# Four of the sixteen up units of a block as seven products of sums, in a fused retention and MLP kernel

## The chip, the cores and the metric

The kernel runs on one core of a Trainium2 chip. The metric is the device time of one execution in microseconds (us), lower is better. Its engines, each with its own queue of instructions in a fixed order: TensorE (PE in the profile; PEld are its weight loads), VectorE (DVE), ScalarE (ACT), GpSimd (POOL) and SyncE (SP), which here only issues DMA transfers.

## The reference

Retention over 8 batches, 8 heads, 576 steps of 64 features, and behind it an MLP with a hardswish on the 4608 rows that come out. Cut to what matters:

```python
scores = scale * np.matmul(q, k.transpose(0, 1, 3, 2))
Dmat = np.where(rel >= 0, gamma[:, None, None] ** rel[None, :, :], 0.0)
ret = np.matmul(scores * Dmat[None], v)
x = ret.transpose(0, 2, 1, 3).reshape(B * S, H * D)      # 4608 x 512
h = x @ w_in                                             # 512 x 2048
g = h * np.clip(h + 3.0, 0.0, 6.0) / 6.0
out = g @ w_out                                          # 2048 x 512
```

## The kernel before

The rows are worked off in nine blocks of 512 (block 0 gathers the first 64 steps of every batch, blocks 1 to 8 are the rest of one batch each). A block has three parts of work on TensorE:

- Attention, in chunks of 128 rows, in 64 x 64 tiles. It gives the block's transposed input `xts[kb]`, 512 features x 512 rows, in f16. Chunks have steps with letters: `c` casts a chunk's k, q and v to f16 (k on ScalarE, q and v on GpSimd, L188 to L195), then issues the transposing DMAs and the loads of a later chunk on SP's queue; `a` scores, `s` state sums, `u` adds to the running state (two additions on VectorE, L313 and L316, then a scaling by GpSimd, L317), `z` casts a state to f16 on ScalarE (L323), `x` and `i` multiply and copy the result into `xts`.
- Up: 16 units. A unit is 128 of the 2048 columns of h for all 512 rows: 4 products of 512 columns (`up_steps`, L491). Its result lies in one PSUM bank; ScalarE makes u = relu(h/6 + 0.5) from it (L510), and VectorE g = min(u, 1) * h (L512).
- Down: from block 2 on (`down_strassen`, L562) the product with w_out is made by the scheme of Strassen in Winograd's form: 7 products of half the size in each direction instead of 8, from sums of parts of g (side sums, L527, on VectorE, taken from a list by the step `+`) and sums of parts of w_out that are made once (`ws`). This comes to 112 TensorE products of 256 columns a block. The results of the seven are copied from PSUM by ScalarE or combined by VectorE and GpSimd; two of the banks take a second product on top of the first once the first has been copied. The copy that the prediction follows is `nc.scalar.copy(u2, bc)` (L631 before, L712 in the changed kernel), after down product 6 and before down product 7 is added to the same bank.

What `product` issues is two matmuls, one for each half of the 128 output partitions, so a product is two matmul instructions in the profile.

The order of instructions is written out by hand. In the loop over kb from 2 (L811) the up units of block kb + 1, the down products of block kb and the attention steps for later blocks are interleaved: before unit 0 come 5 down products, behind each unit 7 (less those that were taken ahead), and a table by unit number, `STEADY` (L710), says which steps stand behind which unit: for instance 4 chunk c4 is cast; behind 5 come 7 more down products and the steps a2, x0, s2, i0, u2; c6 stands behind 12, z3 behind 8. `FIRST_STEADY` does so for kb = 2.

[...] An instruction on any engine waits, in order, until the bank or buffer that it writes is free.

At the start, before data has come, TensorE runs idle products (`idle_products`, L375): 11 products of 512 columns on the identity, in four groups between the first transposes.

Of the kernel before, what the change touches and what calls it, by code (L numbers as in the profile page):

```python
# [21 lines left out]
def kernel(  # L22
# [21 lines left out]
    JQ = 4  # L44
    HB = BLK // 2
    FIRST = 2
    HM = DM // 2
# [39 lines left out]
    zh = [const.tile([P, NP, D], FP32, name=f"zh{b}") for b in range(B)]  # L87
# [61 lines left out]
    def product(out, lhs, rhs, **flags):  # L149

        for h2 in range(2):
            r = slice(h2 * D, h2 * D + D)
            nc.tensor.matmul(out[r], lhs[:, r], rhs, skip_group_check=True, **flags)  # L153
# [333 lines left out]
    def up_unit(kb, u, th=None):  # L487
        for _ in up_steps(kb, u, th):
            pass
# [47 lines left out]

    def out_tile(kb, m2):
        return work.tile([P, 2, DM], FP32, tag=f"o{m2}", bufs=2, name=f"o{m2}_{kb}")

    kept = deque()

# [149 lines left out]
    def go(plan, kb=None, down=None):  # L692
# [3 lines left out]
        for item in plan.split():  # L696
# [9 lines left out]
            else:  # L706
# [3 lines left out]
    STEADY = {0: [("u", 1)], 1: [("z", 1), ("+", 1)], 2: [("+", 1)], 4: [("c", 4)],  # L710
# [4 lines left out]

# [6 lines left out]

    with tc.manual_schedule(engines={ENG.PE, ENG.DVE, ENG.Pool, ENG.Activation, ENG.SP}):
# [25 lines left out]
        idle_products(5)  # L749
# [5 lines left out]
        idle_products(4)  # L755
# [9 lines left out]
        idle_products(1)  # L765
# [4 lines left out]
        idle_products(1)  # L770
# [24 lines left out]
        for u in range(4, NFC):  # L795
# [14 lines left out]
           2, down)  # L810
        for kb in range(2, NB):  # L811
            for _ in down:
                pass
            plain = kb < FIRST
            down = down_plain(kb) if plain else down_strassen(kb)
            per = 4 if plain else 7
            table = FIRST_STEADY if kb == 2 else STEADY
            c = NCB * (kb + 2)
            owed = 0
            for u in range(NFC):  # L820
                if u == 0:
                    owed += per - 2
                    for _ in range(per - 2):
# [5 lines left out]
                owed -= per  # L829
                while owed < 0:  # L830
                    next(down, None)
                    owed += 1
                for w, i in table.get(u, []):
                    if w == "D":
                        for _ in range(i):
                            next(down, None)
                        owed += i
                    else:
                        do([(w, i if w == "+" else c + i)])
# [32 lines left out]
```

## Time and profile before

| what | value |
|---|---|
| median of three runs | 299.51 us (298.39 to 301.02) |
| the profiled execution | 301.02 us |
| its span, first to last instruction | 299.3 us |
| granted TensorE clock, mean | 1.000 |
| TensorE, busy from 180 to 200 us | 20.00 of 20.00 us |
| VectorE, the same stretch | 14.36 us |
| ScalarE, the same stretch | 13.33 us |
| GpSimd, the same stretch | 8.96 us |
| TensorE, busy from 0 to 20 us | 15.63 us |

The profile is of one execution, the longest of the three. A group of instructions is named by its line, engine and operation, what it writes and reads, and its shape (partitions x elements and type); behind the bar stand its busy time, the mean duration of one instruction in ns, and the idle time of the engine just before, with what ended it. In a timeline the first two numbers are the start and the length in us; in the chain of waits too, where each piece is a stretch of work that the end of the run was waiting for. Matmuls are pipelined, and their ends are modelled.

### The profile page before, as it was taken

How to read it: one execution, taken by the hardware profiler on the slowest of the kernel's cores; microseconds unless marked ns; L12 is line 12 of the kernel's file. 1: busy time of each engine (PE TensorE's matmuls, PEld its weight loads, DVE VectorE, ACT ScalarE, POOL GpSimd, SP SyncE). 2: the span in 40 equal slices, each digit the busy share in tenths (PEclk: the TensorE clock that was granted, in tenths of full speed). 3: DMA queues.
4: the chain of work that ended last, by engine and by line, in shares of the span. 5: the costliest groups of instructions: out<-in, count | busy, mean ns of one | idle time of the engine just before them, and what ended most of it. 6: DMA issues, size and time to landing. Idle time of an engine off the chain costs nothing.

```text
span 299.3 us, 12661 instructions
## 1 busy us (share of the span) xinstructions
PE 287.4 (96%) x5574; PEld 219.3 (73%) x5574; DVE 216.2 (72%) x388; ACT 193.9 (65%) x360; POOL 133.7 (45%) x170
## 2 busy tenths in 40 slices
PE   4999998999999999999999999999999999999995
PEld 2776644777556667888777878778778987778894
DVE  7749545669897778788967797688869776647654
ACT  3748854799866696686677577667766574565420
POOL 8971057526762920719631962386247003100510
PEclk9999999999999999999999999999999999999999
DMA  6999999998999999997999999999906100200114
GB/s 157 157 182 213 186 227 209 227 228 183 161 216 164 249 202 191 178 239 195 225 220 225 169 201 216 150 177 247 148 3 142 72 2 30 102 15 2 72 72 140
DMA packets 119542, 47.86 MB, mean 160 GB/s; under 512 B 92352, under 2 KB 114880, under 8 KB 119488
## 3 DMA queue, kind: packets, MB, share of 16 engines
q1 hardware_dynamic: 114336, 41.56, 71.1%
q0 software_dynamic: 4720, 5.11, 10.5%
q8 instruction: 43, 0.70, 1.0%
q10 hardware_dynamic: 432, 0.39, 0.5%
q14 instruction: 11, 0.09, 0.1%
HBM read 36.70 MB, written 9.44 MB: 154 GB/s over the span
## 4 chain that ended last, share of the span: by engine, by line
PE 79%; DMA 9%; POOL 6%; SPq 2%; ACT 2%; issue 1%; DVE 1%; POOLq 0%; ACTq 0%
PE ph L153 37%; PE pm L153 29%; DMA wout<-in_moe_w_out_dram 6%; PE pd L153 5%; PE po L231 4%; DMA fq<-in_q_dram 2%; PE pa L231 2%; SPq L174 2%; POOL hv L439 1%; POOL hk L399 1%; POOL win L658 1%; PE pu L231 1%; POOL ws L741 1%; PE ptk L153 1%; POOL q L192 1%
## 5 line engine op out<-in xcount | busy, mean ns | idle before, releaser
L153 PE MATMUL ph<-xT,win 128*64 128x512 f16 (+1 forms) x1248 | 144.8, 364 | 1.2 <-DMA win<-in_moe_w_in_dram 0.5
L512 DVE SCALAR_TENSOR_TENSOR g<-u,ph 128x512 f16<-128x512 f32 (+1 forms) x156 | 98.8, 643 | 53.1 <-ACT u L510 52.6
L510 ACT ACTIVATE u<-ph,half 128x512 f32<-128x512 f32 (+1 forms) x156 | 100.5, 659 | 43.0 <-PE ph L153 40.6
L153 PEld LDWEIGHTS <-win 128*64 128x64 f16 x1248 | 82.9, 136 | 28.6 <-DMA win<-in_moe_w_in_dram 1.1
L153 PEld LDWEIGHTS <-g 128*64 128x64 f16 x928 | 51.1, 110 | 14.9 <-issue 0.4
L153 PEld LDWEIGHTS <-s 128*64 128x64 f16 x896 | 50.3, 110 | 8.1 <-issue 0.2
L317 POOL TENSOR_TENSOR z<-z,gpow 128x256 f32<-128x256 f32 x24 | 15.8, 657 | 69.1 <-DVE z L316 51.2
L153 PE MATMUL pm<-ws,s 128*64 128x256 f16 x672 | 45.6, 273 | 0.0
L192 POOL TENSOR_TENSOR q<-fq,dec 128x512 f16<-128x512 f32 x32 | 36.7, 1166 | 3.4 <-DVE zh L282 1.7
L369 ACT CAST xT<-po 128x256 f16<-128x256 f32 (+1 forms) x44 | 22.5, 583 | 23.4 <-PE po L231 22.5
L195 POOL TENSOR_TENSOR v<-fv,dec 128x512 f16<-128x512 f32 x32 | 35.4, 1111 | 2.1 <-DMA fv<-in_v_dram 2.1
L591 POOL TENSOR_TENSOR u<-u,p 128x512 f32<-128x512 f32 x7 | 8.9, 1271 | 60.4 <-ACT u L631 54.2
L153 PE MATMUL pd<-wout,g 128*64 128x512 f16 x256 | 34.7, 382 | 0.1
L153 PE MATMUL pm<-wout,g 128*64 128x256 f16 x448 | 31.1, 273 | 0.0
L266 DVE TENSOR_TENSOR a<-pa,mask 128x256 f16<-128x256 f32 (+1 forms) x44 | 21.9, 539 | 8.4 <-PE pa L231 4.7
L188 ACT CAST k<-fk 128x512 f16<-128x512 f32 x32 | 19.9, 622 | 2.1 <-DMA fk<-in_k_dram 2.1
L527 DVE TENSOR_TENSOR s<-g 128x1024 f16<-128x1024 f16 x28 | 19.3, 692 | 0.2
L323 ACT CAST z<-z 128x512 f16<-128x512 f32 x24 | 14.9, 622 | 5.1 <-DVE z L313 4.7
L153 PE MATMUL pm<-ws,g 128*64 128x256 f16 x224 | 16.7, 274 | 0.0
L153 PE MATMUL pm<-wout,s 128*64 128x256 f16 x224 | 16.3, 273 | 0.1
L527 DVE TENSOR_TENSOR s<-g,s 128x1024 f16<-128x1024 f16 x14 | 13.3, 949 | 0.0
L231 PE MATMUL po<-qT,z 64*64 64x64 f16 x512 | 12.5, 198 | 0.4 <-ACT z L326 0.3
(106 smaller groups left out, 270.0 us busy)
## 6 DMA issues: line engine op xcount, KB each, us to landing
fk<-in_k_dram SPq DMA_DIRECT2D x32, 256.0 KB, 4.6
fq<-in_q_dram SPq DMA_DIRECT2D x16, 512.0 KB, 6.0
fv<-in_v_dram SPq DMA_DIRECT2D x32, 256.0 KB, 5.5
out_dram<-o SPq DMA_DIRECT2D x14, 512.0 KB, 3.8
wout<-in_moe_w_out_dram POOLq DMA_DIRECT2D x4, 512.0 KB, 17.9
out_dram<-o SPq DMA_DIRECT2D x7, 256.0 KB, 5.4
win<-in_moe_w_in_dram POOLq DMA_DIRECT2D x3, 512.0 KB, 10.9
hq<-in_q_dram SPq DMA_DIRECT2D x6, 128.0 KB, 4.6
```

The source lines that it names most:

```text
L153: nc.tensor.matmul(out[r], lhs[:, r], rhs, skip_group_check=True, **flags)
L188: nc.scalar.copy(by_head(k16), in_rows(st[c]["fk"]))
L192: nc.gpsimd.tensor_tensor(by_head(q16[:, e]), in_rows(st[c]["fq"][:, :, e, :]), in_rows(dd[:, 2 + e, 0:H, :]), ALU.mult)
L195: nc.gpsimd.tensor_tensor(v16, st[c]["fv"], dd[:, 1, H:2 * H, :], ALU.mult)
L231: return lambda: nc.tensor.matmul(*args, skip_group_check=True, **flags)
L266: nc.vector.tensor_tensor(a16[:, a, 0:n].rearrange("p x i q -> p (x i) q"), pa[a].rearrange("p x i q -> p (x i) q"), m, ALU.mult)
L317: nc.gpsimd.tensor_tensor(new, new, decay, ALU.mult)
L323: nc.scalar.copy(z16, zs[c])
L369: nc.scalar.copy(xt[:, s], po[s].rearrange("p x n (e r) -> p x n e r", e=2))
L510: nc.scalar.activation(uu[:, 0:n], ph[:, 0:n], ACTF.Relu, bias=half, scale=1.0 / 6.0)
L512: nc.vector.scalar_tensor_tensor(out=g[:, hf, ths, jr, :], in0=by_half(uu), scalar=1.0, in1=by_half(ph), op0=ALU.min, op1=ALU.mult)
L527: nc.vector.tensor_tensor(*pend.popleft())
```

## The change

From kb = 3 to kb = 7, that is for the up parts of blocks 4 to 8, units 8 to 11 (the first four with `jq` = 1) are made together, as a quad. The 512 x 512 part of w_in and the 512 x 512 input are each cut in 2 x 2, and the seven products of Strassen's method in Winograd's form take the place of the eight block products. Each of the seven is four products of 256 columns. The 64 products of 512 columns of a block's up part become 48 of 512 and 28 of 256.

- `sums_of_w` makes four sums of parts of w_in once, on GpSimd, behind unit 14 of kb = 2 (step `W`). They lie in a part of `wout16` that is no longer read.
- `sums_of_x` makes four sums of parts of `xts` in each of the five blocks, on GpSimd (step `T`, behind u1 and z1).
- `up_quad` is a generator with six stretches, called by `Q1` and five times `q` in `PLAN`, which takes the place of the table `STEADY` for these blocks. It uses three banks (x, z, y), of which x and y are added to after they have been copied to `p` and `q` in SBUF by ScalarE.
- In the order, c6 moves from behind unit 12 to behind the first stretch of the quad, and z3 from behind unit 8 to behind the fifth, and the side sums move among the new stretches.
- The first of the two output tiles has one buffer in place of two, and one tile more of its kind, `late_out`, holds the first output tile of block 1 and then the sums of x. `zh` becomes one tile, of which a part holds `q` of the quad. `query` moves into a tile that exists already.
- The idle products have 80 columns in place of 512, and there are 24, 19, 5 and 5 in place of 5, 4, 1 and 1.
- kb = 2 and kb = 8 keep their order.

```diff
-    query = const.tile([P, P], FP32)
-    dist, far = early[:, 0:P], early[:, P:2 * P]
+    dist, far, query = early[:, 0:P], early[:, P:2 * P], early[:, 2 * P:3 * P]
...
-        idle = psum.tile([P, NP, P], FP32, tag="pp", name="idle")
+        idle = psum.tile([P, 80], FP32, tag="pp", name="idle")
         for _ in range(n):
-            product(idle, ident16, ident16.unsqueeze(1).to_broadcast([P, NP, P]), start=True, stop=True)
+            product(idle, ident16, ident16[:, 0:80], start=True, stop=True)
...
+    late_out = const.tile([P, 2, DM], FP32)
     def out_tile(kb, m2):
-        return work.tile([P, 2, DM], FP32, tag=f"o{m2}", bufs=2, name=f"o{m2}_{kb}")
+        return late_out if (kb, m2) == (1, 0) else work.tile([P, 2, DM], FP32, tag=f"o{m2}", bufs=1 + m2, name=f"o{m2}_{kb}")
...
+    def sums_of_w(jq):
+        w, (s1, s2, s3, s4) = w_of(jq), [w_sums[:, n] for n in range(4)]
+        a11, a12, a21, a22 = [w[:, 2 * k:2 * k + 2, JP * i:JP * i + JP] for i in range(2) for k in range(2)]
+        for o, x, y, op in ((s1, a21, a22, ALU.add), (s2, s1, a11, ALU.subtract), (s3, a11, a21, ALU.subtract),
+                            (s4, a12, s2, ALU.subtract)):
+            for c in range(2):
+                nc.gpsimd.tensor_tensor(o[:, c], x[:, c], y[:, c], op)
+
+    def sums_of_x(kb):
+        b11, b12, b21, b22 = [xts[kb][:, 2 * k:2 * k + 2, HB * t:HB * t + HB] for k in range(2) for t in range(2)]
+        t1, t2, t3, t4 = [x_sums[:, n] for n in range(4)]
+        nc.gpsimd.tensor_tensor(t1, b12, b11, ALU.subtract)
+        nc.gpsimd.tensor_tensor(t2, b22, t1, ALU.subtract)
+        nc.gpsimd.tensor_tensor(t3, b22, b12, ALU.subtract)
+        nc.gpsimd.tensor_tensor(t4, b21, t2, ALU.subtract)
+
+    def gate(kb, g, src):
...
+        nc.scalar.activation(u, src, ACTF.Relu, bias=half, scale=1.0 / 6.0)
+        nc.vector.scalar_tensor_tensor(out=g, in0=u, scalar=1.0, in1=src, op0=ALU.min, op1=ALU.mult)
+
+    def up_quad(kb, jq):
...
+        plain = lambda i, k: (lambda c, j: w[:, 2 * k + c, JP * i + j, :])
+        summed = lambda n: (lambda c, j: w_sums[:, n - 1, c, j, :])
+        x = lambda k, t: (lambda c: xts[kb][:, 2 * k + c, HB * t:HB * t + HB])
+        xs = lambda n: (lambda c: x_sums[:, n - 1, c, :])
...
+        def one(n, lhs, rhs, more=False):
+            for j in range(JP):
+                for c in range(2):
+                    product(b[n][:, j, :], lhs(c, j), rhs(c), start=(c == 0 and j == 0 and not more), stop=(c == 1))
+
+        b["x"] = bank("x")
+        one("x", plain(0, 0), x(0, 0))
+        nc.scalar.copy(p, b["x"])
+        b["z"] = bank("z")
+        one("z", plain(0, 1), x(1, 0))
+        nc.vector.tensor_tensor(b["z"], b["z"], p, ALU.add)
+        yield
+        b["y"] = bank("y")
+        one("y", summed(1), xs(1))
+        nc.scalar.copy(q, b["y"])
+        one("x", summed(2), xs(2), True)
+        nc.scalar.copy(p, b["x"])
+        gate(kb, g[:, 0, 0:JP], b["z"])
+        yield
+        one("y", summed(4), x(1, 1), True)
+        nc.vector.tensor_tensor(b["y"], b["y"], p, ALU.add)
+        yield
+        one("x", summed(3), xs(3), True)
+        nc.scalar.copy(p, b["x"])
+        gate(kb, g[:, 1, 0:JP], b["y"])
+        nc.gpsimd.tensor_tensor(q, q, p, ALU.add)
+        yield
+        one("x", plain(1, 1), xs(4), True)
+        gate(kb, g[:, 0, JP:JQ], b["x"])
+        yield
+        gate(kb, g[:, 1, JP:JQ], q)
+        yield
...
-    STEADY = {0: [("u", 1)], 1: [("z", 1), ("+", 1)], 2: [("+", 1)], 4: [("c", 4)],
-              5: [("D", 7), ("a", 2), ("x", 0), ("s", 2), ("i", 0), ("u", 2)], 6: [("c", 5), ("u", 3), ("+", 1)],
-              7: [("z", 2), ("+", 1)], 8: [("z", 3)], 9: [("+", 1)], 10: [("+", 1)],
-              12: [("c", 6)], 13: [("D", 6), ("a", 4), ("x", 2), ("s", 4), ("i", 2), ("u", 4), ("D", 1)],
-              14: [("c", 7), ("z", 4), ("+", 1)], 15: [("+", 1)]}
+    PLAN = ("D5 U0 D2 u1 U1 D7 z1 T +1 U2 D7 +1 U3 D7 U4 D7 c4 U5 D14 a2 x0 s2 i0 u2 "
+            "U6 c5 u3 +1 U7 D7 z2 +1 Q1 c6 D6 q D7 q +1 D5 q +1 D6 U12 q z3 D9 q U13 D15 a4 x2 s4 i2 u4 D1 "
+            "U14 z4 c7 +1 U15 D7 +1")
...
-        idle_products(5)
+        idle_products(24)
...
+            if SIDE <= kb < NB - 1:
+                steady(kb, down)
+                continue
```

In `PLAN`, `D` is so many down products of block kb, `U` an up unit of block kb + 1, `Q` and `q` the stretches of the quad, `T` the sums of x, and the other letters are the steps above.

More of the change, by code (lines that the diff above doesn't have):

```diff
@@ L86 @@
     gpow = const.tile([P, NP], FP32)
-    zh = [const.tile([P, NP, D], FP32, name=f"zh{b}") for b in range(B)]
+    states_of_heads = const.tile([P, B, NP, D], FP32)
+    zh = [states_of_heads[:, b] for b in range(B)]
     def indices():
@@ new lines, in sums_of_x @@
+    def sums_of_x(kb):
[6 more added lines that the diff above has]
+    def gate(kb, g, src):
+        u = work.tile([P, BLK], FP32, tag="u", bufs=3, name=f"u{kb}")
+        u = u.rearrange("p (j t) -> p j t", j=JP)
+        nc.scalar.activation(u, src, ACTF.Relu, bias=half, scale=1.0 / 6.0)
+        nc.vector.scalar_tensor_tensor(out=g, in0=u, scalar=1.0, in1=src, op0=ALU.min, op1=ALU.mult)
@@ L810, with steady @@
            2, down)
+        def steady(kb, down):
+            c0 = NCB * (kb + 2)
+            u, quad = 0, None
+            for item in PLAN.split():
+                what, n = item[0], int(item[1:] or 0)
+                if what == "D":
+                    for _ in range(n):
+                        next(down, None)
+                elif what == "U":
+                    up_unit(kb + 1, n)
+                elif what == "Q":
+                    quad = up_quad(kb + 1, n)
+                    next(quad)
+                elif what == "q":
+                    next(quad)
+                elif what == "T":
+                    sums_of_x(kb + 1)
+                else:
+                    do([(what, n if what == "+" else c0 + n)])
         for kb in range(2, NB):
@@ L813 @@
                 pass
[L814 to L817, printed above, removed]
+            down = down_strassen(kb)
+            if SIDE <= kb < NB - 1:
+                steady(kb, down)
+                continue
+            table = FIRST_STEADY if kb == 2 else {}
             c = NCB * (kb + 2)
@@ L821 @@
                 if u == 0:
-                    owed += per - 2
-                    for _ in range(per - 2):
+                    owed += 5
+                    for _ in range(5):
                         next(down, None)
@@ L828 @@
                     side_sums(1)
-                owed -= per
+                owed -= 7
                 while owed < 0:
```

23 lines of the change are left out of this document (20 added, 3 removed), and 2 rows, old and new, of the table FIRST_STEADY.

## The prediction

> **What bounds the kernel now.** I read the page first, for the busy shares:
>
> ```profile
> PE 287.4 (96%) x5574; PEld 219.3 (73%) x5574; DVE 216.2 (72%) x388; ACT 193.9 (65%) x360; POOL 133.7 (45%) x170
> ```
>
> TensorE is busy nearly all the time, and no other engine comes near it. Busy is not the same as paced, so I read the chain of waits next, inside the stretch that the change rewrites (start, length, what):
>
> ```profile
> 213.35 0.76 PE pm L153 x14
> 214.12 0.86 PE ph L153 x8
> 214.98 0.77 PE pm L153 x14
> 215.74 0.86 PE ph L153 x8
> ```
>
> From 72 us to 294 us the chain is almost nothing but such pieces, end to end: an up unit (8 matmuls, 4 products of 512 columns) takes 0.864 us, seven down products of 256 columns take 0.765 us. So a product costs 0.216 us at 512 columns and 0.1093 us at 256. What is taken off TensorE here comes off the end, and each microsecond in which TensorE waits is added. The chain before 50 us runs through GpSimd's DMA issues, the w_out transfer and the q load, not through TensorE.
>
> Third, the timeline where the quad is put (block kb = 5; the first unit that it replaces starts at 213.95, my t = 0), ScalarE, VectorE and GpSimd by themselves:
>
> ```profile
> 212.76 0.69 ACT L510 ACTIVATE u<-ph,half 128x512 f32<-128x512 f32 x1
> 213.33 0.62 ACT L188 CAST k<-fk 128x512 f16<-128x512 f32 x1
> 213.84 0.70 ACT L510 ACTIVATE u<-ph,half 128x512 f32<-128x512 f32 x1
> 214.42 0.63 ACT L323 CAST z<-z 128x512 f16<-128x512 f32 x1
> ```
>
> ```profile
> 214.09 0.42 DVE L313 TENSOR_TENSOR z<-pu,z 128x256 f32<-128x256 f32 x1
> 214.42 0.68 DVE L527 TENSOR_TENSOR s<-g 128x1024 f16<-128x1024 f16 x1
> 215.02 0.68 DVE L512 SCALAR_TENSOR_TENSOR g<-u,ph 128x512 f16<-128x512 f32 x1
> 215.62 0.69 DVE L527 TENSOR_TENSOR s<-g 128x1024 f16<-128x1024 f16 x1
> 216.22 0.68 DVE L512 SCALAR_TENSOR_TENSOR g<-u,ph 128x512 f16<-128x512 f32 x1
> ```
>
> ```profile
> 212.83 0.61 POOL L317 TENSOR_TENSOR z<-z,gpow 128x256 f32<-128x256 f32 x1 [3.99 <-DVE z L316]
> ```
>
> ScalarE and VectorE work off a queue here: the relu at 213.84 belongs to a unit whose matmuls were done at 213.35. Back to back, an instruction starts before the one ahead of it ends, by 0.12 us on ScalarE (a relu of 0.69 is followed after 0.57) and 0.09 on VectorE (0.69, after 0.60).
>
> Fourth, the groups that price the steps (count, then busy us and mean ns of one):
>
> ```profile
> L195 POOL TENSOR_TENSOR v<-fv,dec 128x512 f16<-128x512 f32 x32 | 35.4, 1111 | 2.1 <-DMA fv<-in_v_dram 2.1
> ...
> L591 POOL TENSOR_TENSOR u<-u,p 128x512 f32<-128x512 f32 x7 | 8.9, 1271 | 60.4 <-ACT u L631 54.2 <-ACT u L603 6.2
> ...
> L591 DVE TENSOR_TENSOR u<-pm,p 128x512 f32<-128x512 f32 x6 | 4.1, 685 | 0.1
> ...
> L631 ACT COPY u<-pm 128x512 f32<-128x512 f32 x6 | 3.5, 577 | 0.0
> ```
>
> **What comes off TensorE.** A quad replaces 16 products of 512 columns by 28 of 256, in five blocks (kb = 3 to 7). Old: 16 x 0.216 = 3.46 us. New at the row of the down products: 28 x 0.1093 = 3.06, a gain of 0.40. Twelve of the 28 read w_in with a stride; the only strided products of 256 columns (48 matmuls from 64.54, 2.84 us, less 0.27 for the last) come to 0.112, runs of 24 to 0.114. At 0.113 the quad is 3.11 and the gain 0.35. I take 0.35, five times: 1.75 us; the ends are 1.4 (everything at 0.114, with two bank changes) and 1.98.
>
> [...]
>
> **What the quad hangs on.** Its sums pass through PSUM copies, and TensorE may add to a bank again only when ScalarE has copied it. Per quad ScalarE gets four copies (0.58 each), VectorE two additions (0.685), GpSimd four sums of x and one addition. All of this lies beside TensorE's work unless TensorE meets it. I follow one quad from t = 0, with 0.04 us from a matmul's end to ScalarE, 0.03 from ScalarE to VectorE and 0.05 to TensorE.
>
> - TensorE: x 0 to 0.44, z to 0.87, six down products to 1.53, y to 1.97, x again to 2.40, seven to 3.17, y again to 3.61, five to 4.15, x to 4.59, six to 5.25, unit 12 to 6.11, x for the last time to 6.55.
> - VectorE works off what it has: the addition to z starts where 216.22 stood, 2.27, and ends at 2.96.
> - ScalarE: copy of x 0.98, the cast of chunk c6 (moved forward) to 2.10, copy of y from 2.17, second copy of x from 2.99 (it overwrites what the addition to z reads), relu of z 3.45 to 4.14.
> - VectorE: gate of z 4.17 to 4.85, addition to y 4.78 to 5.46, for it stands behind the gate.
> - ScalarE: third copy of x 5.50, relu of y 5.96, relu of unit 12 6.53, relu of x 7.10, the cast z3 7.67, and only then the copy of down product 6 into u2, 8.17 to 8.75.
>
> Down product 7 accumulates on that bank. TensorE has eight products of down product 4 in between and comes to it at 6.57 + 0.87 = 7.44; it may go at 8.80. **It waits 1.36 us.** Before, a whole unit and eight products covered that copy, and z3 stood four units earlier. Everything behind it on TensorE (unit 13, the next attention group) moves with it.
>
> The floor holds without any queue: after x, drain and release 0.20, relu 0.57, z3 0.50, copy 0.58 and release 0.05 make 1.90, less 0.87 of cover: 1.03 us; 0.53 in kb = 7, which has no attention and no z3. With its own starts (addition to z at 1.70, nothing of c6 and z3) kb = 7 comes to 0.67 by the same steps.
>
> **GpSimd.** The four sums of x stand behind u1's scaling, ahead of the three instructions of c4 and of u2's scaling (L317), which had 3.99 us of idle time ahead of it. Nothing in the trace adds two f16 tensors of this size there; from below 1.04 (the smallest of L195), from above 1.27 (L591) or 1.49 (L195 with VectorE busy beside it). I take 1.11, L195's mean, its output and size being the same: 4.44 us. Scaling then ends 0.45 us later, and VectorE's L313, which started 0.65 after it, does not notice. At 1.27 it slips 0.44, at 1.49 1.3, and the wait grows by as much. In kb = 3 the eight sums of w come first: 256 elements, L317's 0.613, 4.9 us from 143.33. Then scaling 0.61, sums 4.44, c4 (2 x 1.17 and 1.11) and scaling 0.61: 157.33, where L313 started at 156.01. That block waits 1.32 more. c6's three instructions now stand ahead of the quad's own GpSimd addition; from 0.5 us on they take 3.4 to 4.4 and end by 4.9, and the addition's operand comes only at 6.08.
>
> [...] Trace: the side sum L527 takes 0.69 beside an idle GpSimd and up to 1.16 beside L195, which then takes 1.50. [...]
>
> **Edits that cost nothing.** Narrow idle products: four cold products of 128 columns took 0.43 us, so 24 of 80 take 1.6 to 2.6 us where 2.34 stood; TensorE then idled 1.94 us for hk, and the chain there is GpSimd's. If that cover were gone, 0.3 us. One buffer for the first output tile: its store is issued some 80 products before the next write, and lands in 3.8 to 5.4 us. c6 forward: its transposes and loads pass a store on SP's queue; the steady stretch shows one wait of 0.2 us for a transpose.
>
> **Sum.** Waits: kb = 3 2.68, kb = 4 to 6 1.36 each, kb = 7 0.67, together 7.43; less 1.75: +5.7 us. The profiled execution took 301.0 us (span 299.3) and would become 306.7; it was the longest of three, and on the median of 299.5 that is **305.2 us**.
>
> **Rivals.**
> - GpSimd decides. Its sums at 1.27 and c4's pair at the contended 2.94: the scaling slips 2.57 in kb = 3 and 0.44 in kb = 4 and 5, waits 9.6, 307.3 us; at 1.49 for the sums and for c4's v, 3.8 and 1.3, 310.3 us. For it: the trace has such instructions; against: the median is 1.04.
> - Only the floor: 4 x 1.03 + 0.53 = 4.65, less 1.98, 302.2 us. For it: VectorE's queue may be shorter once TensorE waits; against: the gate of z ahead of the addition to y.
> - The wait is hidden and the gain remains: 299.5 - 1.75 = 297.8 us, not slower. It decides if the copy to u2 ends within 0.87 us of the last x product, that is if ScalarE had 1.03 us less to do. Against it stand the three ScalarE rows; for it only that ends of matmuls are modelled.
>
> **How the numbers follow.** Forecast 0.64, GpSimd 0.15, floor 0.11, hidden 0.10. The range 301.5 to 309.0 leaves out the hidden case and the far end of GpSimd. One per cent, about what a measurement here can tell from no change, is 3 us: 296.5 to 302.5 counts as the same. A gain over 3 us exceeds all that comes off TensorE: 0.03. The hidden case and most of the floor fall within: 0.19. Slower: 0.78.
>
> **What would show it.** In the changed profile: down product 7 on TensorE waiting for ScalarE's copy L712, over 1 us in kb = 3 to 6, less in kb = 7; quad matmuls at 0.109 to 0.114 a pair; GpSimd's x sums near 1.1 us; the first 50 us as before. No such wait, or TensorE stopped at x or y by copies instead, would make the forecast wrong.

## The result and the profile after

The changed kernel takes **309.87 us** (median of four, 309.20 to 310.60) against 299.73 us of the kernel before on the same chip (298.39 to 301.02). The ratio is 1.0339, 95% interval 1.0283 to 1.0395: slower, by 10.1 us where 5.7 was forecast. The profiled execution took 309.23 us (span 307.4). Its first page, busy shares and the chain of waits by engine:

```profile
PE 286.6 (93%) x5778; PEld 227.1 (74%) x5778; DVE 227.9 (74%) x398; ACT 202.8 (66%) x380; POOL 173.8 (57%) x203
...
PE 56%; POOL 11%; ACT 10%; DVE 8%; DMA 8%; issue 5%; SPq 1%; ACTq 0%; POOLq 0%
```

TensorE has 0.8 us less to do in a span 8.1 us longer, and 29% of the chain now runs through GpSimd, ScalarE and VectorE (9% before). What TensorE waits for, from 112 to 302 us (us in total, times, longest):

```profile
PE pm L153 <- ACT u L712: 5.4, 5, 1.2
PE pm L153 <- issue: 2.1, 1, 2.1
PE pq_x L153 <- ACT part L614: 1.4, 3, 0.5
PE pq_x L153 <- ACT part L607: 1.0, 2, 0.7
```

The first row is the wait of the forecast, once in each of the five blocks. The other three rows are not in it; L607 and L614 are ScalarE's second and third copy of the quad's x bank. The place of the forecast in kb = 4, ScalarE and TensorE in the timeline:

```profile
195.01 0.69 ACT L574 ACTIVATE u<-pq_y,half 128x512 f32<-128x512 f32 x1
195.60 0.69 ACT L510 ACTIVATE u<-ph,half 128x512 f32<-128x512 f32 x1
196.17 0.70 ACT L574 ACTIVATE u<-pq_x,half 128x512 f32<-128x512 f32 x1
196.73 0.64 ACT L323 CAST z<-z 128x512 f16<-128x512 f32 x1
197.24 0.61 ACT L712 COPY u<-pm 128x512 f32<-128x512 f32 x1
```

```profile
195.17 0.66 PE L153 MATMUL pq_x<-late_out,win 128*64 128x256 f16 x8 [0.47 <-ACT part L614]
195.66 1.04 PE L153 MATMUL pm<-ws,g 128*64 128x256 f16 x16
197.91 0.30 PE L153 MATMUL pm<-ws,s 128*64 128x256 f16 x2 [1.21 <-ACT u L712]
```

The queue on ScalarE is the one that was forecast, instruction by instruction: relu of y, of unit 12, of x, the cast z3, then the copy. The brackets count idle time from the modelled end of the matmul before; from start to start the step takes 1.48 us where 0.11 is normal, so the wait is 1.37 us.

A measure that leaves the start out (up to the second attention group of kb = 3 the profiled executions of the table took 149.9 to 152.1 us): the time between the starts of TensorE's attention groups. From the second group of a block to its fourth is the stretch that holds the quad.

| kernel | kb = 3 | kb = 4 | kb = 5 | second group of kb = 3 to the end |
|---|---|---|---|---|
| before | 14.59 | 14.39 | 14.38 | 147.45 |
| changed | 19.28 | 16.45 | 16.14 | 157.06 |
| e1 copy first | 18.21 | 14.95 | 14.95 | 153.59 |
| e2 z3 last | 18.78 | 15.67 | 15.67 | 154.93 |
| e3 sums behind | 17.41 | 15.19 | 15.19 | 157.47 |
| e4 no x sums | 19.28 | 16.78 | 16.78 | 158.05 |
| e5 c6 back | 19.06 | 16.63 | 16.34 | 157.24 |
| e6 w early | 16.98 | 16.46 | 16.04 | 154.83 |
| e7 wide idle | 19.52 | 16.19 | 16.15 | 157.32 |
| e8 together | 15.85 | 14.71 | 15.11 | 150.86 |
| e9 pauses filled | 15.86 | 13.93 | 13.93 | 148.30 |
| e12 before, narrow idle | 15.89 | 14.38 | 14.89 | 148.99 |

The changed kernel loses 9.61 us behind that point: 4.69 in kb = 3, 2.06 and 1.76 in the next two stretches, 1.53 from there on, less 0.43 in the stretches between.

Why TensorE waits for L607 and L614 as well is seen on VectorE and GpSimd, kb = 4, where t = 0 of the forecast is 188.00:

```profile
188.25 0.42 DVE L313 TENSOR_TENSOR z<-pu,z 128x256 f32<-128x256 f32 x1
188.59 1.18 DVE L527 TENSOR_TENSOR s<-g 128x1024 f16<-128x1024 f16 x1
189.69 0.68 DVE L512 SCALAR_TENSOR_TENSOR g<-u,ph 128x512 f16<-128x512 f32 x1
190.29 0.93 DVE L527 TENSOR_TENSOR s<-g 128x1024 f16<-128x1024 f16 x1
191.14 0.69 DVE L601 TENSOR_TENSOR pq_z<-pq_z,part 128x512 f32<-128x512 f32 x1
```

```profile
188.17 1.04 POOL L195 TENSOR_TENSOR v<-fv,dec 128x512 f16<-128x512 f32 x1
189.18 2.94 POOL L192 TENSOR_TENSOR q<-fq,dec 128x512 f16<-128x512 f32 x2
```

The two side sums (L527) were forecast at 0.69 us each and took 1.18 and 0.93, beside GpSimd's instructions of c5 (L195) and c6 (L192). The addition to z (L601) starts at t = 3.14 where 2.27 was forecast, and the copies behind it are as late: L607 and L614 then stop TensorE for 0.41 and 0.64 us.

And kb = 3, GpSimd (L561 are the sums of w_in) and VectorE, then TensorE:

```profile
141.79 2.11 POOL L561 TENSOR_TENSOR wout<-win 128x256 f16<-128x256 f16 x2
143.85 1.32 POOL L561 TENSOR_TENSOR wout<-wout,win 128x256 f16<-128x256 f16 x2
145.13 1.63 POOL L561 TENSOR_TENSOR wout<-win 128x256 f16<-128x256 f16 x2
146.72 1.75 POOL L561 TENSOR_TENSOR wout<-win,wout 128x256 f16<-128x256 f16 x2
...
156.58 0.61 POOL L317 TENSOR_TENSOR z<-z,gpow 128x256 f32<-128x256 f32 x1
```

```profile
157.23 0.42 DVE L313 TENSOR_TENSOR z<-pu,z 128x256 f32<-128x256 f32 x1 [2.77 <-POOL z L317]
```

```profile
153.37 0.60 PE L153 MATMUL pm<-wout,s 128*64 128x256 f16 x7
156.03 0.62 PE L153 MATMUL pm<-wout,s 128*64 128x256 f16 x7 [2.06 <-issue]
```

The sums of w_in took 6.7 us from 141.79, where 4.9 was forecast. VectorE stood for GpSimd's scaling 2.77 us. And TensorE stopped for 2.06 us in the middle of a group of 14 matmuls that all read what was long there: "issue" means that the trace shows nothing it waited for.

### The profile page after: what moved, and what is told of

Read it like the earlier page. It is cut to its first block, busy times and chain, and to the rows that moved or that the text cites. A ratio compares the mean times of both kernels' runs of the same rounds, so it can differ in the third digit from the quotient of the medians.

```text
span 307.4 us, 13138 instructions
## 1 busy us (share of the span) xinstructions
PE 286.6 (93%) x5778; PEld 227.1 (74%) x5778; DVE 227.9 (74%) x398; ACT 202.8 (66%) x380; POOL 173.8 (57%) x203
## 4 chain that ended last, share of the span: by engine, by line
PE 56%; POOL 11%; ACT 10%; DVE 8%; DMA 8%; issue 5%; SPq 1%; ACTq 0%; POOLq 0%
PE ph L153 24%; PE pm L153 19%; PE pd L153 6%; DMA wout<-in_moe_w_out_dram 6%; PE po L231 3%; ACT u L574 2%; PE pa L231 2%; DMA fk<-in_k_dram 2%; DVE s L527 2%; POOL wout L561 2%; DVE g L512 2%; ACT u L510 2%; POOL hv L439 1%; POOL q L192 1%; POOL hk L399 1%
## 5 line engine op out<-in xcount | busy, mean ns | idle before, releaser
L153 PE MATMUL ph<-xT,win 128*64 128x512 f16 (+1 forms) x1088 | 123.3, 362 | 0.7 <-ACT xT L369 0.4
L512 DVE SCALAR_TENSOR_TENSOR g<-u,ph 128x512 f16<-128x512 f32 (+1 forms) x136 | 84.6, 636 | 34.7 <-ACT u L510 33.6
L510 ACT ACTIVATE u<-ph,half 128x512 f32<-128x512 f32 (+1 forms) x136 | 86.6, 656 | 29.3 <-PE ph L153 25.8
L153 PEld LDWEIGHTS <-win 128*64 128x64 f16 x1208 | 80.2, 136 | 26.2 <-ACT part L614 3.2
L317 POOL TENSOR_TENSOR z<-z,gpow 128x256 f32<-128x256 f32 x24 | 15.8, 657 | 55.4 <-DVE z L316 40.0
L192 POOL TENSOR_TENSOR q<-fq,dec 128x512 f16<-128x512 f32 x32 | 36.7, 1168 | 1.6 <-PE pu L231 1.3
L195 POOL TENSOR_TENSOR v<-fv,dec 128x512 f16<-128x512 f32 x32 | 35.6, 1118 | 1.5 <-DMA fv<-in_v_dram 1.4
L266 DVE TENSOR_TENSOR a<-pa,mask 128x256 f16<-128x256 f32 (+1 forms) x44 | 21.9, 540 | 9.1 <-PE pa L231 6.1
L527 DVE TENSOR_TENSOR s<-g 128x1024 f16<-128x1024 f16 x28 | 21.8, 781 | 0.2
L616 POOL TENSOR_TENSOR states_of_heads<-states_of_heads,part 128x512 f32<-128x512 f32 x5 | 6.4, 1273 | 27.5 <-ACT part L614 27.5
L672 POOL TENSOR_TENSOR u<-u,p 128x512 f32<-128x512 f32 x7 | 8.9, 1272 | 17.6 <-ACT u L712 11.3
L153 PE MATMUL pm<-ws,g 128*64 128x256 f16 x224 | 15.8, 274 | 0.0
L527 DVE TENSOR_TENSOR s<-g,s 128x1024 f16<-128x1024 f16 x14 | 14.0, 1004 | 0.0
```

The costliest lines, as they stand in the source:

```text
L192: nc.gpsimd.tensor_tensor(by_head(q16[:, e]), in_rows(st[c]["fq"][:, :, e, :]), in_rows(dd[:, 2 + e, 0:H, :]), ALU.mult)
L195: nc.gpsimd.tensor_tensor(v16, st[c]["fv"], dd[:, 1, H:2 * H, :], ALU.mult)
L266: nc.vector.tensor_tensor(a16[:, a, 0:n].rearrange("p x i q -> p (x i) q"), pa[a].rearrange("p x i q -> p (x i) q"), m, ALU.mult)
L317: nc.gpsimd.tensor_tensor(new, new, decay, ALU.mult)
L510: nc.scalar.activation(uu[:, 0:n], ph[:, 0:n], ACTF.Relu, bias=half, scale=1.0 / 6.0)
L512: nc.vector.scalar_tensor_tensor(out=g[:, hf, ths, jr, :], in0=by_half(uu), scalar=1.0, in1=by_half(ph), op0=ALU.min, op1=ALU.mult)
```

## The experiments

Three questions: does the L712 queue make its wait, why are the side sums slow, and what makes kb = 3 so long. The kernel before, measured with each experiment, took 300.2 to 301.2 us (medians) there and 299.7 above, so the ratios compare better than the times.

### The order at the end of the quad

**e1** issues one more down product ahead of the last stretch, and with it the copy L712.

```diff
-... D6 U12 q z3 D9 q U13 ...
+... D6 U12 D1 q z3 D8 q U13 ...
```

> One down product is moved from behind the fifth stretch of the quad to ahead of it, so that ScalarE's copy of down product 6 (L712) is issued ahead of the relu of x and the cast z3. Theory A (the wait that was forecast): the wait for L712 goes in all five blocks, 5.4 us in the rows of waits and about 6.2 with the drains, 309.9 becomes 303.7; the waits for L607 and L614, 4.6 us and more in the rows, stay. Theory B (ScalarE and VectorE are simply behind, and TensorE would meet the next copy instead): above 308, with a new wait behind product 7.

**e2** moves only the cast z3 behind the copy.

```diff
-... U12 q z3 D9 q U13 ...
+... U12 q D9 q z3 U13 ...
```

> Only the cast z3 is moved, from ahead of the copy L712 to behind the quad's last stretch. Theory A: ScalarE's steps add up, so the wait for L712 falls by one cast, 0.50 us, from 1.21 to 0.7 in kb = 3 to 6 and not at all in kb = 7, together 2.0 us: 307.9. Theory B: the wait is not a sum of ScalarE's steps, and stays at 1.2: 309.9.

e2 took 307.22 us, ratio 1.0203 (1.0153 to 1.0253): the wait for L712 falls by 0.52 us in kb = 3 to 6 and not in kb = 7, which has no z3.

```profile
PE pm L153 <- ACT u L712: 3.3, 5, 0.7
```

e1 took 306.66 us, ratio 1.0175 (1.0126 to 1.0225). Its waits of TensorE:

```profile
PE pu L231 <- DVE g L512: 1.7, 3, 0.6
PE pq_x L153 <- ACT part L614: 1.1, 3, 0.4
PE pm L153 <- ACT u L712: 0.9, 4, 0.2
```

L712 falls from 5.4 to 0.9 us, so the queue on ScalarE is the cause of that wait. The time lies between theory A's 303.7 us and the 308 and more of theory B, for 1.7 us come in one step on: the fourth attention group needs the bank of unit 13 (the tag `pp` hands six banks out in turn to up units and attention), and VectorE is late with its gate:

```profile
198.69 1.56 DVE L575 SCALAR_TENSOR_TENSOR g<-u,states_of_heads 128x512 f16<-128x512 f32 x1 [0.29 <-ACT u L574]
200.17 0.67 DVE L512 SCALAR_TENSOR_TENSOR g<-u,ph 128x512 f16<-128x512 f32 x1
```

The gate of q (L575) reads two operands in SBUF (the other gates read one in PSUM) and takes 1.56 us beside GpSimd's L672, a combination of down results, not 0.68.

### Side sums and GpSimd

**e3** moves two side sums from the head of the quad to its end.

```diff
-U6 c5 u3 +1 U7 D7 z2 +1 Q1 c6 D6 q D7 q +1 D5 q +1 D6 U12 q z3 D9 q U13
+U6 c5 u3 U7 D7 z2 Q1 c6 D6 q D7 q +1 D5 q +1 D6 U12 q z3 D9 +1 q +1 U13
```

> The two side sums that VectorE makes ahead of the quad's first addition move behind the second and third stretch, and the two after them behind the sixth. Theory A (VectorE's queue delays the addition to z, and through it the copies L607 and L614): the addition to z starts within 1.3 us of the quad's first product where it now takes 3.1 in kb = 4; the waits for L607 and L614 go, about 3.5 us with the drains, and the wait for L712 falls to its floor of 1.03: 309.9 becomes 305 to 306. Theory B (GpSimd's lateness sets it, through the scaling that VectorE waits for): in kb = 3 nothing changes, and in all less than 1.5 us.

310.54 us, ratio 1.0328 (1.0260 to 1.0397), where theory A had 305 to 306. The waits for L607 and L614 are gone, as expected; the time is not, since VectorE now does the same work beside L672 (in kb = 4 a side sum takes 1.61 us there and the gate of q 1.75), and the wait for L712 is still 1.1 us long:

```profile
PE pm L153 <- ACT u L712: 4.8, 5, 1.1
PE pu L231 <- DVE g L512: 4.3, 3, 1.4
```

**e4** makes the sums of x for kb = 3 only (the later blocks multiply old sums; that part of the computation is left out), to see whether they make GpSimd late and the side sums slow.

```diff
-                    sums_of_x(kb + 1)
+                    if kb == SIDE:
+                        sums_of_x(kb + 1)
```

> The sums of x are made for kb = 3 alone; in the four later blocks the quad multiplies the sums of block 4, so that part of the computation is left out and the output is not the reference's. Theory A (the sums make GpSimd late, its work for c5 and c6 then lies beside the side sums and slows them): the side sums ahead of the quad take 0.69 again instead of 1.18 and 0.93 in kb = 4 and 5, the wait for L607 goes there and that for L614 falls below 0.2, 309.9 becomes 308.2. Theory B (the side sums are slow for another reason): within 0.5 us of 309.9. The wait of 1.2 for L712 stays in both.

310.71 us, ratio 1.0316 (1.0265 to 1.0366): no faster. In kb = 4 GpSimd now has 3.77 us of idle time ahead of its scaling, and yet the side sum is slower:

```profile
187.83 1.05 POOL L195 TENSOR_TENSOR v<-fv,dec 128x512 f16<-128x512 f32 x1
188.83 2.49 POOL L192 TENSOR_TENSOR q<-fq,dec 128x512 f16<-128x512 f32 x2
```

```profile
188.85 1.58 DVE L527 TENSOR_TENSOR s<-g 128x1024 f16<-128x1024 f16 x1
190.35 0.67 DVE L512 SCALAR_TENSOR_TENSOR g<-u,ph 128x512 f16<-128x512 f32 x1
190.95 0.93 DVE L527 TENSOR_TENSOR s<-g 128x1024 f16<-128x1024 f16 x1
```

So the theory with which e4 went in, that the sums of x alone are to blame, falls. Without them c5's v is out of the way in time (it ends 0.52 us behind the start of the quad, 0.49 in the kernel before in kb = 5, 1.21 in the changed one), but then c6's two q follow at once, and the side sum meets those.

**e5** puts c6 back behind the quad.

```diff
-Q1 c6 D6 q ... U12 q z3 D9 q U13
+Q1 D6 q ... U12 q z3 D9 q c6 U13
```

> Chunk c6 (three GpSimd instructions, one cast on ScalarE, its loads) goes back behind the last stretch of the quad; nothing else changes. In the changed kernel the two side sums (L527) at the head of a quad take 1.18 and 0.93 us in kb = 4 where the forecast had 0.69, the addition to z starts 0.87 us late, and TensorE waits about 1.05 us for the copies L607 and L614 in kb = 4 (issue terms). Theory A (GpSimd instructions beside the side sums slow them): with c6 away the second side sum takes about 0.69, the first one still meets the v of c5 and stays near 1; the addition to z comes 0.3 to 0.5 us earlier, the two waits together fall by as much, and the wait for L712 stays at 1.2 to 1.4 us: 0.3 to 0.5 us less in each of kb = 3 to 6, 308.0 to 309.0 us in all. Theory B (VectorE is late for another reason, its own queue): the side sums and both waits stay within 0.1 us, 309.9 us.

309.76 us, ratio 1.0282 (1.0248 to 1.0316). VectorE in kb = 4:

```profile
188.70 0.43 DVE L313 TENSOR_TENSOR z<-pu,z 128x256 f32<-128x256 f32 x1 [0.45 <-POOL z L317]
189.04 1.17 DVE L527 TENSOR_TENSOR s<-g 128x1024 f16<-128x1024 f16 x1
190.73 0.68 DVE L527 TENSOR_TENSOR s<-g 128x1024 f16<-128x1024 f16 x1
```

The second side sum fell from 0.93 to 0.68 us, the first stayed at 1.17, beside the v of c5, which the sums of x make late: theory A for the cause, and with e4 each of the two edits is enough for a slow side sum. For the time theory A fails: the addition to z starts 0.19 us later than in the changed kernel instead of earlier, for c6's three instructions now stand ahead of the later ones on GpSimd, its scaling (L317) ends 0.45 us later, and VectorE waits for that in front of the first side sum. The gain is paid back on the other engine. The ratio is lower than the changed kernel's 1.0339, but the intervals overlap, and neither kb = 4 nor kb = 5 is shorter in the table.

### kb = 3

**e6** makes the sums of w_in behind unit 5 of kb = 2, **e7** takes the old, wide idle products at the start.

```diff
-                    ... 5: [("t", 3), ("c", 5)],
+                    ... 5: [("t", 3), ("c", 5), ("W", 1)],
...
-                    14: [("z", 4), ("c", 7), ("+", 1), ("W", 1)], 15: [("+", 1)]}
+                    14: [("z", 4), ("c", 7), ("+", 1)], 15: [("+", 1)]}
```

> The sums of w_in (16 instructions on GpSimd, 6.7 us of it in the changed kernel) are made nine units earlier, behind unit 5 of kb = 2. The number and order of TensorE's instructions do not change. In the changed kernel the stretch of kb = 3 from the second to the fourth attention group takes 19.28 us, 2.83 more than that of kb = 4, and 2.06 us of it is a stop in the middle of a group of down products that the trace puts down to issue. Theory G (both come from GpSimd being late): kb = 3 becomes like kb = 4, 16.4 us, the stop is gone, 307.0 us. Theory F (the stop is a late fetch of TensorE's own instructions, which stands at the same place in the program): the stop of 1.4 to 2.3 us stays at the same product, only 0.5 to 0.8 us of kb = 3 goes, 309.2 us.

> The idle products as they were: 11 of 512 columns instead of 53 of 80 columns, 42 products fewer ahead of everything else on TensorE. Theory F (the stop of 2.06 us in kb = 3 is a late fetch of TensorE's instructions, which come in blocks of a fixed count): the stop moves 42 products further on in the program, 4.6 to 9 us later, or changes its length or goes. Theory G (GpSimd or a transfer is what TensorE waits for): the stop stays at the same product. For the idle products themselves my forecast was no cost: the first 50 us and the whole then agree with the changed kernel within 0.5 us (309.9 us, or 307.8 if the stop goes with them).

e6: 308.39 us, ratio 1.0229 (1.0188 to 1.0271). kb = 3 falls from 19.28 to 16.98 us, VectorE waits 0.31 us there in place of 2.77, and L607 and L614 do not stop TensorE. But the stop put down to issue stays, at the same product (1.5 us).

e7: 310.28 us, ratio 1.0316 (1.0267 to 1.0364). The stop is gone from that product, with GpSimd's rows at the same times as in the changed kernel to 0.2 us. kb = 3 is no shorter for it; TensorE comes earlier to the copy L607 and waits there, since VectorE still waits for GpSimd:

```profile
157.38 0.42 DVE L313 TENSOR_TENSOR z<-pu,z 128x256 f32<-128x256 f32 x1 [2.09 <-POOL z L317]
```

```profile
161.69 0.66 PE L153 MATMUL pq_x<-late_out,wout 128*64 128x256 f16 x8 [2.26 <-ACT part L607]
```

So up to that wait the stop costs nothing: TensorE goes on at 161.69 us without it and at 161.53 with it, and GpSimd's rows are 0.15 us later in e7. From there to the fourth group e7 takes 8.82 us against 8.08. In this stretch the windows view shows half the granted clock (the number ahead of the last two):

```profile
163.40:165.20 1.80, 1.80 (x14) 0.79 (x10) 1.07 (x3) 1.17 (x2) 0.87 (x1) 0.50 1.13 216
```

The trace has it from 162.15 to 165.56, 3.41 us, up to 1.7 us of work; a part of that lies beneath the waits for L614 and L712. The two runs together part the causes: of the 2.83 us that kb = 3 takes beyond kb = 4, GpSimd's lateness makes 2.3 (e6), and the stop lies beneath it. Neither theory was right alone.

**e12** is one part of the change alone: the kernel before with the 53 narrow idle products.

```diff
-        idle = psum.tile([P, NP, P], FP32, tag="pp", name="idle")
+        idle = psum.tile([P, 80], FP32, tag="pp", name="idle")
...
-        idle_products(5)
+        idle_products(24)
```

> The kernel before with one part of the change alone: 53 idle products of 80 columns for 11 of 512 columns. Forecast for this part: no cost, within 0.5 us of before in the first 50 us and in the whole, 0.998 to 1.002. Theory F (TensorE's instructions come in blocks of a fixed count, and a block that comes late stops it): the 42 products more shift every later block, so that stops put down to issue may come or go, each 0.3 to 2.3 us, with more than 390 TensorE records between the last two fetches; if one comes, up to 1.008. If all blocks come in time, nothing changes.

301.68 us against 300.23, ratio **1.0052** (1.0025 to 1.0079): slower by 1.5 us, with no quad in it. The first 50 us are not to blame, for from the second group of kb = 3 on the table has the same 1.5 us more (148.99 for 147.45); in kb = 3 stands the same stop:

```profile
153.13 0.60 PE L153 MATMUL pm<-wout,s 128*64 128x256 f16 x7
154.85 0.62 PE L153 MATMUL pm<-wout,s 128*64 128x256 f16 x7 [1.12 <-issue]
```

### Together

**e8** has the sums of w_in early, c6 and z3 behind the last stretch and L712 ahead of it. **e9** has the sums of w_in early too, fills VectorE's pauses (behind the addition to z, and behind the one to y) with the side sums, takes L712 ahead of unit 12, and z3 and c6 behind unit 13. **e10** is e9 with wide idle products, **e11** is e9 with unit 13 ahead of the gate of q.

```diff
-U6 c5 u3 +1 U7 D7 z2 +1 Q1 c6 D6 q D7 q +1 D5 q +1 D6 U12 q z3 D9 q U13 D15
+U6 c5 u3 +1 U7 D7 z2 +1 Q1 D6 q D7 q +1 D5 q +1 D6 U12 D1 q D8 q z3 c6 U13 D15    (e8)
+U6 c5 u3 U7 D7 z2 Q1 +1 +1 D6 q D7 q +1 D5 q D7 U12 q D7 q U13 z3 c6 D16          (e9; one +1 behind U4 D7)
+U6 c5 u3 U7 D7 z2 Q1 +1 +1 D6 q D7 q +1 D5 q D7 U12 q D7 U13 q z3 c6 D16          (e11)
```

> Three edits together: the sums of w_in behind unit 5 of kb = 2, chunk c6 and the cast z3 behind the last stretch of the quad, and down product 6 (with its copy L712) issued ahead of that stretch. Each was seen or is tried alone. Theory: the waits lie in a row on the same chain (side sum, addition to z, copies, L712, then the bank of unit 13), so they add as long as each engine keeps up. L712 falls from 1.37 to at most 0.4 us a quad, c6 gives 0.3 to 0.5, a wait of 0.6 to 0.8 for VectorE's gate L512 comes in behind unit 13, and kb = 3 loses 0.6 (stop stays) or 2.6 (stop goes): 304.5 to 306.5 us. Rival (VectorE has too much to do in this stretch, whatever the order): as with the copy alone, 306 to 307.5 us.

> On top of the sums of w_in behind unit 5 of kb = 2: the copy L712 goes ahead of unit 12's relu (one more down product ahead of that unit), the casts z3 and c6 behind unit 13's relu, and the side sums out of the head of the quad into the pauses that VectorE makes there anyway (1.30 us behind the addition to z, 0.73 behind the addition to y), one of them behind unit 4. Theory (the losses of the quad are the order of the queues alone): no wait for L712, L607, L614 or the bank of unit 13 over 0.3 us, kb = 4 to 6 take 14.3 to 14.6 us from the second to the fourth attention group against 14.4 before and 16.1 to 16.5 in the changed kernel, kb = 3 takes 15.0 to 16.0 with its stop of 1.7 us, the rest of before's work unchanged: 0.995 to 1.005 of before. Rival (VectorE and ScalarE have more to do in this stretch than TensorE): a wait of 0.4 us or more stays in each block at one of the four places, 1.006 to 1.012 of before, as with the three edits together (1.0059).

> The same with the idle products as they were (42 products fewer at the head of TensorE's program). If the stop of 1.7 us in kb = 3 depends on the place in TensorE's program, as the run with wide idle products alone says, it is not at that product here, and with GpSimd no longer late its end is not taken over by another wait: 0.5 to 1.7 us less than with narrow ones, 0.990 to 1.002 of before. If it comes from something else in that block, the two agree within 0.5 us.

> The last kernel but one (side sums in the pauses, L712 ahead of unit 12) with unit 13 ahead of the gate of q, which takes 1.6 us on VectorE beside GpSimd's L672 and, standing ahead of unit 13's gate, keeps TensorE waiting 0.47 to 0.49 us for that unit's bank in each of kb = 2 to 5. Theory (order of VectorE's queue): the wait is under 0.15 us in kb = 3 to 5, 1.0 to 1.5 us off the whole, 0.995 to 1.000 of before. Rival (VectorE is simply late there, and the mask L266 behind the gate of q is next): a wait of as much stands at the products that need the masked scores, time as before this edit, 1.002. What remains in either case are the stops put down to issue, 1.6 us in kb = 3 and others.

| kernel | median us | ratio to before (95%) |
|---|---|---|
| e8 | 302.90 | 1.0059 (1.0037 to 1.0082) |
| e9 | 301.72 | 1.0022 (0.9994 to 1.0049) |
| e10 | 302.45 | 1.0060 (1.0030 to 1.0089) |
| e11 | 301.89 | 1.0048 (1.0026 to 1.0069) |

e8 was better than its theory's 304.5 to 306.5 us. In e9 the quad's waits are all gone, and the stretch with the quad takes 13.93 us, less than before's 14.39. Its waits of TensorE, then VectorE in kb = 5:

```profile
PE pm L153 <- issue: 1.3, 1, 1.3
PE pu L231 <- DVE g L512: 1.0, 4, 0.3
PE po L231 <- issue: 0.4, 1, 0.4
```

```profile
216.45 0.70 DVE L601 TENSOR_TENSOR pq_z<-pq_z,part 128x512 f32<-128x512 f32 x1
217.06 1.28 DVE L527 TENSOR_TENSOR s<-g 128x1024 f16<-128x1024 f16 x2
218.70 0.69 DVE L575 SCALAR_TENSOR_TENSOR g<-u,pq_z 128x512 f16<-128x512 f32 x1 [0.35 <-ACT u L574]
```

Two side sums in 1.28 us, with GpSimd idle, in a pause that was there anyway. What remains in e9 is a step of 0.47 to 0.49 us, from start to start, at the bank of unit 13 in kb = 3 to 5 (the gate of q, 1.61 us beside L672), and the stops. e11 bears out its rival: with the gate of q later the mask L266 is late, TensorE waits for it twice, 0.4 us in all, and the time is no shorter. e10's stop in kb = 3 is gone, but others come, 0.46, 0.89, 1.06 and 1.29 us, and it is no faster; half of its expectation fails.

**e13, e14, e15** are e9 with 42, 32 and 21 narrow idle products in place of 53, all else the same.

> The kernel with the side sums in the pauses (53 idle products; 1.0022 of before, stops put down to issue of 1.60 and 0.63 us in its profile), with 42 idle products of 80 columns: all later instructions of TensorE move up by 11 products. Theory F: stops come at other products and with other lengths, each behind a stretch with more than 390 TensorE records between two fetches or 200 and more since the last one; the stretches between attention groups that hold no stop stay as they were to 0.1 us, and the time differs from that kernel by the difference of the stops, 0.993 to 1.006 of before. Rival (the stops belong to a product and its data): 1.60 us at the same product of kb = 3.

> As the one before, with 32 idle products: 21 products up. The same theories: stops at other places, 0.993 to 1.006 of before, or the same 1.60 us in kb = 3.

> As the one before, with 21 idle products: 32 products up. The same theories: stops at other places, 0.993 to 1.006 of before, or the same 1.60 us in kb = 3. If in one of the three the stops come to under 0.5 us in all, the gain of the quads is free and that one is 0.993 to 0.997 of before.

Ratios 1.0044 (1.0013 to 1.0076), 1.0124 (1.0073 to 1.0176), 1.0062 (1.0032 to 1.0091). The stops move: with 42 the one of kb = 3 is 1.33 us and stands 11 products on, before an up unit; with 32 and 21 it is not there, and others come (0.94, 1.16 and 0.89 us with 32; 1.72 us with 21). Theory F holds for the place, while the time with 32 lies above its range of 0.993 to 1.006; that a lucky count frees the quads' gain was not met in these counts. Where the stops lie was counted out of the trace, as the number of TensorE's records (weight loads, matmuls and the some 20 instructions of its queue that are neither) from the start of the execution:

```
kernel     stop us   records ahead of it       = 256 x n + 193
before     0.41      8897                      34
changed    2.33      6081                      23
e6         1.77      6081                      23
e7         0.38 0.51 0.37  4801 5313 8385      18 20 32
e8         1.66 0.86 6081 6593                 23 25
e9         1.60 0.63 6081 7873                 23 30
e10        0.46 0.89 1.06 1.29  4801 6593 7105 8385   18 25 27 32
e12        1.39 0.57 6081 8385                 23 32
e13        1.33 0.81 0.74  6081 6593 7873      23 25 30
e14        0.94 1.16 0.37 0.89  5313 6593 8385 9153   20 25 32 35
e15        1.72      8385                      32
```

(Stops of more than 0.35 us put down to issue, from start to start, 100 to 290 us; in e7 the stretch at half the granted clock is left out.) All of them stand at the same place in a block of 256 records. e1 to e5 and e11 have the stop at 6081 too, of 1.47 to 2.18 us.

## Why the prediction was right, and where it was wrong

**Right: the direction, the mechanism and its price.** Down product 7 waits for ScalarE's copy L712: 1.37 us in kb = 4 and 5 for 1.36 forecast, 0.72 in kb = 7 for 0.67. The copy of x starts at t = 0.99 (0.98), that of y at 2.17 (2.17). e1 and e2 show the queue to be the cause. So the forecast stands for what it looked at. By stretches, against its waits less the gain: 4.69 us for 2.33 in kb = 3, 2.06 for 1.01 in kb = 4, 1.76 for 1.01 in kb = 5, 1.20 for 1.01 in kb = 6 and 0.32 for 0.32 in kb = 7. The missing 4.4 us lie in kb = 3 to 5, in two terms that it put too small; a third hardly shows in this kernel.

Two sizes were off without weight. A quad takes TensorE 3.06 us where no product of it waits (kb = 7, and all five in e9), a gain of 0.40 and not 0.35: the 48 strided matmuls that gave 0.112 are 24 products, and from the first start to the last, 47 steps, they take 2.57 us, 0.109 a product. The sums of x take 1.14 to 1.16 us each in kb = 3 (1.11 forecast), but from kb = 4 on two of the four take 1.49 to 1.61 us, each begun under a side sum of VectorE, and the four come to 5.4 us for 4.44.

**"The addition to z starts where 216.22 stood, 2.27."** This step failed, by 0.87 us in kb = 4. It took VectorE's timeline of before as it stood, and GpSimd was idle beside it there. But the change itself moves c6 to this place, and the sums of x push c5's v into it. The text had the collision (1.16 for a side sum beside L195, 1.50 for L195) and charged it to GpSimd alone, as a rival. It falls on VectorE, ahead of an addition on which the quad hangs: 1.05 us more in kb = 4, 0.64 in kb = 5, and in kb = 3 the addition to z starts as late behind L313 as in kb = 4 (2.89 us). The price stood in the trace of before, and 1.16 was not its end: there a side sum takes up to 1.40 us beside L195 and 1.73 beside L591. e5 shows c6's share in the second side sum; e9, with the sums where GpSimd is idle, shows the waits gone.

**"eight sums of w ..., L317's 0.613, 4.9 us."** They took 6.7. In e6, where no side sum stands beside them, they take 0.61 to 0.84 us each and 5.3 in all; in the changed kernel three of the eight take 1.05 to 1.30 us beside side sums. So most of the error is the same collision, seen from GpSimd. Relative to the second attention group of kb = 3 the scaling ended 1.36 us later than forecast. With the side sums this makes kb = 3: 2.68 us of waits forecast, plus 1.05, plus 1.4, is 5.1; measured 5.1 (4.69 + 0.40). e6 takes 2.3 of it away.

**"Edits that cost nothing. Narrow idle products."** Their own time costs nothing, as forecast. But 42 products more at the head move every later instruction of TensorE, and that alone makes the kernel before 1.5 us slower (e12). The prediction priced an instruction by its duration only. In the changed kernel this loss lies beneath GpSimd's in kb = 3 (e7) and comes out once that is mended (e6, e8, e9).

**The rivals.** "GpSimd decides" put the slip of kb = 3 at 2.57 us, and 2.68 was measured, but by luck: it gave it to the sums of x, which were near their forecast there, and not to the sums of w. That its two times, 307.3 and 310.3, enclose the measured one is luck too. "Only the floor" and "hidden" are out: TensorE waited more than the forecast, not less. That VectorE becomes late, in front of z and again in front of unit 13, was not among them, and e1 and e3 show that this stands right behind the forecast wait.

**Can the change pay?** In e9 the quad stretches are 0.46 us shorter than before's, more than the gain that was forecast, and the whole is the same as before: 0.32 us of it goes to the gate of q behind each of kb = 3 to 5 (14.95 for 14.63 behind kb = 3), and the rest to the stops. Of 15 kernels none was shown faster than the kernel before. Left open: a gate of q that does not read two operands in SBUF beside L672, and a program whose blocks all come in time.

## What to carry to other kernels

When an edit moves GpSimd work, ask which VectorE instructions with two operands in SBUF will now stand beside it, price those by what the traces show (here they ended 0.55 us after the GpSimd instruction), and follow what hangs on them; do not take their places from the old timeline. Fill an engine's known pauses with the work that nothing waits for, instead of moving it ahead of or behind the step that counts. And an edit that changes the number of TensorE instructions early in a program of thousands must be measured by itself, as in e12, before a gain or loss of 0.5% is put down to anything else.

## What the runs showed of the hardware

**A side sum that meets a GpSimd instruction ends 0.55 us after it.** One that starts while a GpSimd instruction runs ends 0.55 us after that instruction ends: 189.77 behind 189.22 in the changed kernel, 220.49 behind 219.94 in its kb = 5, 190.21 behind 189.66 in e5; the gate of q in e9 ends at 225.19 behind 224.64. In the kernel before, 20 of the 23 additions at L527 that begin so end 0.547 to 0.553 us after it; the other three began within its last 0.04 us and took 0.68 to 0.69. Apart from such late starts the 17 traces have some 590 of these instructions (0.54 to 0.59 us). Taken alone a side sum needs 0.68 to 0.69. That reads as if it stood until the other was done; beside the same GpSimd work the gates L512 on 512 columns, with one operand in PSUM, keep their 0.67 to 0.69. In e4 the side sum (188.85 to 190.43) fits the first of the two q, which began 0.02 us ahead of it, and not the v, which ended 0.03 us after its start.

**TensorE's instructions come in blocks of 256.** The trace has a DMA queue for instructions with 45 transfers of 16 KB in the changed kernel, for 11,556 weight loads and matmuls, which is 257 a transfer (43 for 11,148 in the kernel before). In the changed kernel none started between 143.76 and 153.60 us, while TensorE worked through 472 records; it stopped at 153.97 and went on at 156.03, 1.4 us after that transfer had landed (154.63). Every stop listed above stands 193 records behind a multiple of 256, in kernels with and without quads and with five counts of idle products. And the n-th transfer fits record 256 x n + 193 throughout: at some 490 such places in the 17 traces, from 100 to 290 us, TensorE never began that record less than 1.20 us after the landing, and at the 31 steps of more than 0.35 us among them it began 1.21 to 1.61 us after. One of these the view puts down to ScalarE, 0.66 us at 189.00 in kb = 4 of e5. So a stop goes with a block that came late; why the transfer started late was not found, and the position of a stop could not be foretold.

**A stretch at half the clock.** In e7 TensorE stood for 2.26 us, and 0.46 us after it went on the granted clock fell to 0.50 for 3.41 us; the mean over that execution is 0.994, against 0.997 to 1.000 in the profiled executions of the other 16 kernels. In the changed kernel the stop of 2.33 us from start to start, up to 156.03, has none behind it: the granted clock is 1.00 from 150 to 170 us. That the wait in e7 caused it is not shown.
